# One slot pool, identity-matmul score sums, column-wise layer norm and kept V tiles in a four-layer decode attention kernel

## Chip, cores and metric

The kernel runs on one core of a Trainium2 chip. The metric is the device time of one execution in microseconds (us), as the median of several runs; lower is better. Engines in the profile: PE is TensorE (PEld its weight loads), DVE is VectorE, ACT is ScalarE, POOL is GpSimd, SP is the engine that issues the transfers (SPq its queue). I number layers 1 to 4 and heads 0 to 31; K31 is the K tile of head 31.

## The reference, cut to what matters

```python
# B = Sq = 1, D = 640, 32 heads, 8192 keys, head size 192, bf16
def block(x, k_cache, v_cache, wq, wo):
    q = (x @ wq).reshape(32, 192)
    p = softmax(einsum("hd,hkd->hk", q, k_cache) * 192 ** -0.5)
    return einsum("hk,hkd->hd", p, v_cache).reshape(1, 6144) @ wo
for w in (A, B, A, B):                       # two sets of caches and weights, each used twice
    x = x + block(layernorm(x), *w)
```

A K or V tile of one head is 8192 x 192 bf16, 3.146 MB. Four layers of 32 heads read 256 such tiles and 62.9 MB of Wq and Wo, 868.2 MB in all. Nothing can be reused within a layer, but layers 3 and 4 read the same K and V as layers 1 and 2.

## The kernel before

A tile lies in SBUF as 128 partitions of 64 keys x 192. DVE multiplies the K tile by q, then halves it by adds (192 to 96, 48, 24, 12) for 56 of the 64 key columns and reduces the rest; ACT sums the other 8. PE does the softmax's small transposes and 64 matmuls with V. There are three slots for K, three for V, and two buffers each for Wq and Wo.

```python
e = DV.op(lambda v: v.tensor_tensor(k3, k3, qb_ap, ALU.mult))            # L463, whole tile
...
e = DV.op(lambda v: v.tensor_tensor(kt[:, :, 0:hw_], kt[:, :, 0:hw_], kt[:, :, hw_:DH], ALU.add))   # L492, then L504 x3
...
cur["s"] = DV.op(lambda v: v.tensor_reduce(s_sb[par][:, JA:JJ], kt[:, :, 0:w], AX.X, ALU.add))      # L508
...
for j in range(JJ):                                                       # L557, 64 matmuls with V
    t.matmul(OB[par][0:1, 0:DH], lhsT=p_sb[par][:, j:j + 1], rhs=vs3[:, j, :], ...)
...
# order of the transfers, head by head: K runs one head ahead of V
need_k(h); need_k(h + 1); need_k(h + cfg.get("klead", max(1, NKSLOT - 2))); need_v(h)
...
# weights: rows of 2,048 bytes (Wq, 1,024 columns) and of 1,280 bytes (Wo)
WQ[:, c0:c0 + ncols].rearrange("(c p) n -> p c n", p=128)
WO[r0:r0 + NT * 128, :].rearrange("(t p) n -> p t n", p=128)
```

## Time and profile before

2,074.88 us (2,074.28 to 2,074.90, three runs); the profiled execution spans 2,073.2 us.

From the page of the kernel before: the span, busy time by engine, the rows in 40 slices for PE's granted clock (tenths), the DMA engines (tenths busy) and their rate, then the data queue and the bytes read.

```profile
span 2073.2 us, 24389 instructions
PE 1158.3 (56%) x9625; PEld 915.1 (44%) x9668; DVE 1764.8 (85%) x1190; ACT 596.1 (29%) x3254; POOL 3.1 (0%) x13
PEclk7777777877678777777767777777776777777877
DMA  9999999999999999999999999999999999999995
GB/s 395 430 425 428 422 422 427 426 430 419 423 426 425 427 422 424 426 426 428 418 423 426 423 429 424 422 427 426 426 410 425 425 423 424 423 423 425 426 427 254
q1 hardware_dynamic: 77700, 868.24, 99.3%
HBM read 868.22 MB, written 0.00 MB: 419 GB/s over the span
```

The DMA row is full from the first slice to the last but one: the kernel is bound by its transfers. DVE is busy 85% of the time, but the transfers do not run short because of it.

From the table of stretches of the kernel before; the last two columns are the DMA engines' busy share and the rate in GB/s, the number before them is the granted clock.

```profile
900.00:920.00 20.00, 14.07 (x104) 11.03 (x105) 18.95 (x13) 8.10 (x45) 0.00 (x0) 0.67 1.00 430
920.00:940.00 20.00, 13.66 (x124) 10.82 (x122) 15.13 (x12) 5.54 (x31) 0.00 (x0) 0.90 1.01 420
1540.00:1560.00 20.00, 15.36 (x141) 12.24 (x139) 6.26 (x13) 3.99 (x22) 0.00 (x0) 0.84 0.96 394
```

430 GB/s is the rate with K and V alone; with a weight block in the stretch it is 420 at the same busy share, and at a layer end (the third line) it is lower because the queue runs short for a moment. The Trainium skill, "DMA: Bandwidth & Descriptors", Specifications, puts the fabric ceiling at 435 GB/s; the trace agrees with 430.

From the landing of K31 to the end are 2,073.2 - 2,043.45 = 29.7 us.

### The profile page before, as it was taken

What the parts mean: (1) busy time and instruction counts of PE and PEld (TensorE: products, weight loads), DVE (VectorE), ACT (ScalarE), POOL (GpSimd) and SP (SyncE); (2) the same over time, 40 slices, a digit from 0 to 9 for tenths busy, and PEclk for the clock granted to TensorE, in tenths of its full rate; (3) what the DMA queues carried; (4) which work ended last, traced back from release to release, by engine and by line L of the source; (5) the groups of instructions that cost most, each with busy time, mean ns of one, the idle gap of its engine ahead of it and who ended that gap; (6) DMA issues with size and microseconds to landing.
All of it is one profiled execution on the core that took longest, in us unless ns stands there. A gap on an engine that the chain in (4) does not pass through costs nothing.

```text
span 2073.2 us, 24389 instructions
## 1 busy us (share of the span) xinstructions
PE 1158.3 (56%) x9625; PEld 915.1 (44%) x9668; DVE 1764.8 (85%) x1190; ACT 596.1 (29%) x3254; POOL 3.1 (0%) x13
## 2 busy tenths in 40 slices
PE   2565556555465555566536565556563665556656
PEld 1444444444354444444425454445452454444444
DVE  7888888988698888898779888889878988888896
ACT  2222232232232322232223332223222332223232
POOL 0000000000000000000000000000000000000000
PEclk7777777877678777777767777777776777777877
DMA  9999999999999999999999999999999999999995
GB/s 395 430 425 428 422 422 427 426 430 419 423 426 425 427 422 424 426 426 428 418 423 426 423 429 424 422 427 426 426 410 425 425 423 424 423 423 425 426 427 254
DMA packets 77813, 869.79 MB, mean 420 GB/s; under 512 B 4994, under 2 KB 29572, under 8 KB 44932
## 3 DMA queue, kind: packets, MB, share of 16 engines
q1 hardware_dynamic: 77700, 868.24, 99.3%
q8 instruction: 76, 1.25, 0.2%
q14 instruction: 37, 0.30, 0.0%
HBM read 868.22 MB, written 0.00 MB: 419 GB/s over the span
## 4 chain that ended last, share of the span: by engine, by line
DMA 45%; issue 25%; DVE 24%; PE 4%; ACT 1%; SPq 1%; POOL 0%; POOLq 0%; DVEq 0%; ACTq 0%
DMA kslot<-in_B_k_cache_dram 28%; DMA kslot<-in_A_k_cache_dram 17%; DVE kslot L463 12%; DVE kslot L504 5%; DVE kslot L492 4%; PE OB L557 3%; DVE s_sb L508 1%; SPq L312 0%; DVE M_sb L530 0%; DVE m_sb L515 0%; PE QB L412 0%; PE YL L632 0%; ACT p_sb L547 0%; DVE rl_sb L572 0%; SPq L295 0%
## 5 line engine op out<-in xcount | busy, mean ns | idle before, releaser
L463 DVE TENSOR_TENSOR kslot<-kslot,q_sb 128x12288 bf16<-128x12288 bf16 x128 | 839.3, 6557 | 226.2 <-DMA kslot<-in_A_k_cache_dram 116.6
L557 PE MATMUL OB<-vslot,p_sb 128*1 128x192 bf16 x8192 | 951.1, 294 | 84.3 <-ACT p_sb L547 78.6
L557 PEld LDWEIGHTS OB<-vslot,p_sb 128*1 128x1 bf16 x8192 | 809.6, 101 | 205.7 <-ACT p_sb L547 93.5
L539 PE MATMUL SA<-M_bf,ones_bf 1*128 1x1 bf16 x128 | 22.9, 179 | 689.2 <-ACT M_bf L537 689.2
L504 DVE TENSOR_TENSOR kslot<-kslot 128x2688 bf16<-128x2688 bf16 (+2 forms) x384 | 374.4, 975 | 13.3
L492 DVE TENSOR_TENSOR kslot<-kslot 128x5376 bf16<-128x5376 bf16 x128 | 374.7, 2927 | 0.1
L481 ACT ACTIVATE kslot<-kslot 128x192 bf16<-128x192 bf16 x1024 | 355.3, 348 | 22.2 <-DVE kslot L463 22.2
L539 PEld LDWEIGHTS SA<-M_bf,ones_bf 1*128 1x128 bf16 x128 | 12.4, 97 | 725.0 <-ACT M_bf L537 725.0
L537 ACT ACTIVATE M_bf<-M_sb 1x1 bf16<-1x1 f32 x128 | 26.5, 207 | 666.3 <-DVE M_sb L530 666.3
L481 ACT ACTIVATION_READ_ACCUMULATOR kslot<-kslot 128x1 f32 x1024 | 192.1, 188 | 0.0
L508 DVE TENSOR_REDUCE s_sb<-kslot 128x56 f32<-128x672 bf16 x128 | 109.1, 852 | 4.4
L632 PE MATMUL YL<-wo,oT_sb 128*1 128x512 bf16 x256 | 83.0, 378 | 51.8 <-ACT oT_sb L609 31.7
L605 ACT ACTIVATE oT_sb<-OB 128x1 bf16<-128x1 f32 x64 | 11.2, 175 | 310.9 <-PE OB L593 310.9
L608 ACT ACTIVATE oT_sb<-OB 64x1 bf16<-64x1 f32 x64 | 10.9, 170 | 281.0 <-PE OB L597 281.0
L412 PE MATMUL QB<-wq,xT_b 128*128 128x512 bf16 x197 | 57.5, 426 | 11.2 <-issue 6.4
L523 PE MATMUL SA<-ident,m_bf 128*1 128x128 bf16 x128 | 28.2, 221 | 54.5 <-ACT m_bf L520 54.5
L632 PEld LDWEIGHTS YL<-wo,oT_sb 128*1 128x1 bf16 x256 | 20.7, 81 | 79.7 <-ACT oT_sb L609 37.2
L634 PE MATMUL YH<-wo,oT_sb 128*1 128x128 bf16 x256 | 55.9, 218 | 0.0
L425 ACT ACTIVATE q_sb<-QB 128x512 bf16<-128x512 f32 x48 | 28.7, 598 | 93.6 <-PE QB L412 93.6
L578 ACT ACTIVATE orow_bf<-OB,rl_sb 1x192 bf16<-1x192 f32 x128 | 51.0, 399 | 1.7 <-DVE rl_sb L572 1.7
L547 ACT ACTIVATE p_sb<-s_sb,negm_sb 128x64 bf16<-128x64 f32 x128 | 44.8, 350 | 4.1
L530 DVE TENSOR_REDUCE M_sb<-SA 1x1 f32<-1x128 f32 x128 | 34.7, 271 | 12.6 <-PE SA L523 12.6
(50 smaller groups left out, 368.9 us busy)
## 6 DMA issues: line engine op xcount, KB each, us to landing
kslot<-in_A_k_cache_dram SPq DMA_DIRECT2D x64, 3072.0 KB, 32.6
vslot<-in_A_v_cache_dram SPq DMA_DIRECT2D x64, 3072.0 KB, 36.1
kslot<-in_B_k_cache_dram SPq DMA_DIRECT2D x64, 3072.0 KB, 32.6
vslot<-in_B_v_cache_dram SPq DMA_DIRECT2D x64, 3072.0 KB, 36.3
wq<-in_A_wq_dram SPq DMA_DIRECT2D x12, 1280.0 KB, 24.9
wo<-in_A_wo_dram SPq DMA_DIRECT2D x16, 960.0 KB, 38.2
wq<-in_B_wq_dram SPq DMA_DIRECT2D x12, 1280.0 KB, 25.7
wo<-in_B_wo_dram SPq DMA_DIRECT2D x16, 960.0 KB, 38.6
```

Source lines behind the costliest of these rows:

```text
L412: return t.matmul(QB[nb % 2][:, 0:ncols], lhsT=xT_b[:, c, :], rhs=wq_buf[s_][:, c, (nb % 2) * 512:(nb % 2) * 512 + ncols], start=(c == 0), ...
L463: e = DV.op(lambda v, k3=k3, qb_ap=qb_ap: v.tensor_tensor(k3, k3, qb_ap, ALU.mult))
L481: ea = AC.op(lambda a, k3=k3, par=par, j=j: a.activation(k3[:, j, :], k3[:, j, :], ACT.Copy, accum_out=s_sb[par][:, j:j + 1]))
L492: e = DV.op(lambda v, kt=kt, hw_=hw_: v.tensor_tensor(kt[:, :, 0:hw_], kt[:, :, 0:hw_], kt[:, :, hw_:DH], ALU.add))
L504: e = DV.op(lambda v, kt=kt, hw_=hw_, w=w: v.tensor_tensor(kt[:, :, 0:hw_], kt[:, :, 0:hw_], kt[:, :, hw_:w], ALU.add))
L508: cur["s"] = DV.op(lambda v, kt=kt, par=par, w=w, JA=JA: v.tensor_reduce(s_sb[par][:, JA:JJ], kt[:, :, 0:w], AX.X, ALU.add))
L539: cur["negM"] = PE.op(lambda t, par=par: t.matmul(SA[par][:, SA_NEGM:SA_NEGM + 1], lhsT=ones_bf[0:1, 0:128], rhs=M_bf[par][0:1, 0:1], star ...
L547: cur["p"] = AC.op(lambda a, par=par: a.activation(p_sb[par][:], s_sb[par][:], ACT.Exp, bias=negm_sb[par][:], scale=C))
L557: return t.matmul(OB[par][0:1, 0:DH], lhsT=p_sb[par][:, j:j + 1], rhs=vs3[:, j, :], start=(j == 0), stop=(j == JJ - 1))
L578: cur["orow"] = AC.op(lambda a, par=par: a.activation(orow_bf[par][:], OB[par][0:1, 0:DH], ACT.Copy, scale=rl_sb[par][0:1, 0:1]), tag=(f"O ...
L632: return t.matmul(YL[0:1, 0:512], lhsT=lhsT, rhs=rhs[:, 0:512], start=st, stop=sp_)
L634: return t.matmul(YH[0:1, 0:D - 512], lhsT=lhsT, rhs=rhs[:, 512:D], start=st, stop=sp_)
```

## The change

Intent: fewer bytes (four V tiles of the first two layers stay in SBUF for the last two), longer rows for Wq and Wo, less DVE work (scores summed by PE with an identity matrix), a short layer norm in column form, and one pool of eight slots for everything. The whole kernel was rewritten; its core, condensed (cuts marked by three dots, lines in words shortened):

```diff
-kslot x3, vslot x3, wq_buf x2, wo_buf x2
+slot = [sb(f"slot{i}", [P, J * DH], BF16) for i in range(NSLOT)]        # NSLOT = 8
+KEPT_A = (4, 12)        # V tiles of layer 1 kept until layer 3
+KEPT_B = (20, 28)       # V tiles of layer 2 kept until layer 4
+first(("k", l, h))                                                      # order: K_h, V_h, K_h+1, V_h+1
+if l < 2 or h not in kept[l % 2]:
+    first(("v", l, h))
-DV: multiply whole tile, four halving adds, reduce; ACT: 8 row sums
+for c in range(4):                                                      # DVE: four multiplies of 48 columns
+    v.tensor_tensor(k3[:, :, d0:d0 + QD], k3[:, :, d0:d0 + QD], q..., ALU.mult)
+for c in range(4):                                                      # PE: 24 matmuls of 512 columns
+    for r in range(QD // R):
+        t.matmul(S[:, :], lhsT=ident[:], rhs=k3[:, :, d0:d0 + R], start=..., stop=...)
+v.tensor_reduce(s_sb[par][:], S[:].rearrange("p (j r) -> p j r", r=R), AX.X, ALU.add)
-Wq: 1,024 columns per block; Wo: four heads per block, "(t p) n -> p t n"
+Wq: 1,920 columns (ten heads) per block, "(p c) n -> p c n"; Wo: ten heads, "(p i) n -> p (i n)"
+q and the output projection: bursts of 75 pairs of weight load and one-column matmul per ten heads
-layer norm on one row of 640
+layer norm on 128 x 5, sums over partitions by a matmul with ones
... (launch and helpers cut)
```

With R = 8 an identity matmul reads 64 x 8 columns, so it adds eight of the 192 product columns for all 64 keys at once.

## The prediction

> **What bounds it now.** The DMA engines. The page's DMA row reads 9 in every slice but the last, the data queue is busy 99.3% of the span, 868.2 MB are read. In a table of 20 us stretches the rate is 430 GB/s where only K and V move, 411 to 421 where a Wq (1,280 KB, rows of 2 KB) or Wo (960 KB, rows of 1.3 KB) block is among them. The Trainium skill, "DMA: Bandwidth & Descriptors", Specifications, gives a fabric ceiling of 435 GB/s; the trace agrees: 430. DVE (85%) has slack: it waits 213 us for K (wait list). Data flows from 3 to 2,052 us; then a tail of 21 us.
>
> **Removed, added, moved.**
> 1. Bytes: four V tiles are not read again, 4 x 3.146 = 12.6 MB, at 430 GB/s: -29 us, all critical.
> 2. Row sizes: 56 weight transfers cost about 0.5 us each beyond their bytes (20 us at 420 against 430), 27 us in all. Now there are 32, most with rows of 3.8 KB (Wq) or 19 KB (Wo). I estimate 8 us left: -19 us.
> 3. Tail: 29.7 us lie between the last K's landing and the end. Now: multiply (6.6 us) with identity matmuls behind it, softmax, 64 V matmuls (5.4 us in the last head), a short projection: an estimated 21, so -9 us.
> 4. DVE: the halving tree (2.93 + 1.56 + 0.86 + 0.51 us) and ACT's 8 row sums (4.3 us) go; about 8.5 us of DVE per head stay of 13.8. Off the critical path.
> 5. PE gains 24 identity matmuls of 512 columns per head, and about 150 weight-load-and-matmul pairs per ten heads. At full clock: identity 5.2 us, V 5.4, softmax bubble 2.5, the rest 1.5: an estimated 14.6 us per head against 15.6 us of DMA. So PE becomes nearly critical. The Trainium skill, "TensorE: Matmul & The Clock Gate", Part 1, says that idleness of about 3.4 us halves PE's clock; the trace agrees: 64 V matmuls took 8.3 us starting at a granted 0.5 and 5.44 at 1.0. With pauses under 3 us the clock should stay mostly at 1.0; the PEclk row should rise from 7 to about 9.
> 6. Slots: kept tiles leave four of eight slots for streaming from head 28 of layer 2 to head 4 of layer 3, a Wq block among them, just where projection, norm and q are serial (about 8 us of lag). Bursts at heads 10 and 20 hold PE 5 to 10 us. Estimated +8 us of DMA gaps.
>
> **Sum.** 2,075 - 29 - 19 - 9 + 8 = about 2,026; allowing for better overlap at layer ends **2,022 us**, range **2,006 to 2,062**. Chances: faster by over 2% (below 2,033) **0.70**, within 2% **0.20**, slower **0.10**.
>
> **What would show each step.** (1) 855.7 MB read. (2) Rate near 428 GB/s while data flows. (3) Last K to end about 21 us. (4) DVE busy near 1,100 us. (5) PE busy over 85%, PEclk 9 or 10, identity matmuls some 216 ns apart. (6) DMA dips only at layer ends, the third deepest; the chain of waits still mostly K transfers.
>
> **What would make it wrong.** Identity matmuls read columns in 16-byte pieces with a stride of 384 bytes; no trace shows their rate. If it is lower, or the clock falls to half between heads, PE needs 17 to 20 us per head and the time goes to 2,200 us or more, PE in the chain of waits. If four slots are too few, the DMA row shows gaps through layers 2 and 3 and the result is within 2%. If short rows cost less than I read, step 2 gains only some 10 us.

## More of the kernel before

The end of the kernel before, from its timeline: when K31 and the two last V tiles were issued (the second number is the time that issuing took), the multiply of K31 when it had landed, and the output's transfer.

```profile
2010.75 3.14 SPq L312 DMA_DIRECT2D kslot<-in_B_k_cache_dram  x1
2013.93 13.02 SPq L320 DMA_DIRECT2D vslot<-in_B_v_cache_dram  x2
...
2043.45 6.56 DVE L463 TENSOR_TENSOR kslot<-kslot,q_sb 128x12288 bf16<-128x12288 bf16 x1 [0.77 <-DMA kslot<-in_B_k_cache_dram]
...
2071.65 0.26 SPq L708 DMA_DIRECT2D out_dram<-xout_bf  x1
```

Note the order: K31 is issued ahead of **both** V30 and V31.

## The result

2,049.76 us (2,046.69 to 2,052.19, four runs) against 2,074.78: 25 us or 1.2% faster, within 2%. I had forecast 2,022 us, 53 us faster: the result lies inside the range that I gave, but only 25 of the 53 us came. Ratios given below are the mean time of one kernel's runs over that of the other's of the same rounds, so not quite the ratio of the medians that I quote; here 0.9877 with a 95% interval of 0.9863 to 0.9891. The experiments ran in several rounds; the median of the kernel before lies between 2,074.8 and 2,075.6 us in all of them, so medians of different rounds can be compared to about 1 us. The changed kernel itself scatters more, from 2,046.7 to 2,052.2 us.

The page of the changed kernel, the same lines, then two of its groups (busy us, mean ns of one | idle before).

```profile
span 2050.1 us, 30175 instructions
PE 1669.0 (81%) x13970; PEld 1119.8 (55%) x13970; DVE 1031.3 (50%) x1071; ACT 148.5 (7%) x541; POOL 3.1 (0%) x13
PEclk9998998998899899899889989989989998998998
DMA  9999999999999999999989999999999999999994
GB/s 403 430 430 424 431 428 424 430 431 429 424 430 430 426 428 429 414 431 430 393 349 429 430 426 428 429 424 429 428 431 426 429 429 426 429 428 427 430 428 179
q1 hardware_dynamic: 49376, 855.66, 98.0%
HBM read 855.64 MB, written 0.00 MB: 417 GB/s over the span
...
L368 PE MATMUL S<-slot,ident 128*128 128x512 bf16 x3072 | 741.4, 393 | 115.6 <-DVE rl L410 67.2
L402 PE MATMUL O<-slot,p_sb 128*1 128x192 bf16 x8192 | 794.2, 264 | 0.0
```

What was hoped for is there: 12.6 MB less, and the median slice reads 429 instead of 425. But two slices in the middle fall to 393 and 349, and the last reads 179 instead of 254. That is where a good part of the gain went.

From the table of stretches of the changed kernel: one in mid-layer, then the end of layer 2.

```profile
900.00:920.00 20.00, 17.16 (x111) 10.05 (x111) 11.80 (x12) 1.06 (x4) 0.00 (x0) 0.91 1.00 430
1000.00:1020.00 20.00, 10.34 (x53) 4.51 (x51) 8.03 (x8) 1.37 (x5) 0.00 (x0) 0.74 0.84 347
1020.00:1040.00 20.00, 18.10 (x191) 13.78 (x190) 8.18 (x9) 0.85 (x3) 0.00 (x0) 0.83 0.99 410
1040.00:1060.00 20.00, 13.75 (x94) 7.75 (x91) 9.84 (x18) 1.76 (x6) 0.55 (x1) 0.83 0.80 318
1060.00:1080.00 20.00, 18.10 (x214) 14.04 (x213) 8.47 (x9) 1.34 (x5) 0.00 (x0) 0.91 0.85 350
```

The busy share of the DMA engines falls with the rate: they have nothing to do. And the end of the changed kernel, from its timeline.

```profile
1974.91 0.33 SPq L196 DMA_DIRECT2D slot<-in_B_v_cache_dram  x1
1982.53 0.33 SPq L196 DMA_DIRECT2D slot<-in_B_k_cache_dram  x1
1987.90 0.33 SPq L196 DMA_DIRECT2D slot<-in_B_v_cache_dram  x1
...
2019.08 3.16 PE L331 MATMUL YB<-oT,slot 128*128 128x1 bf16 x75 [0.28 <-ACT oT L326]
2019.14 1.76 DVE L354 TENSOR_TENSOR slot<-slot,q_sb 128x3072 bf16<-128x3072 bf16 x1 [2.05 <-DMA slot<-in_B_k_cache_dram]
...
2022.17 8.04 PE L402 MATMUL O<-slot,p_sb 128*1 128x192 bf16 x64
2030.14 5.35 PE L368 MATMUL S<-slot,ident 128*128 128x512 bf16 x24
2037.68 7.09 PE L402 MATMUL O<-slot,p_sb 128*1 128x192 bf16 x64
2047.03 0.35 SPq L433 DMA_DIRECT2D out_dram<-x_bf  x1
```

Now V30 is issued ahead of K31. K31 lands at 2,019.1; PE is in the third output projection, then does V30 (8.04 us), and comes to K31's identity matmuls only at 2,030.1. The last landing of K is followed by 31.0 us.

### Where the time lies: one account for all runs

To compare traces I count the time that is lost against 430 GB/s. A stretch of t us that moves b MB loses t - b/0.430. The span is then the bytes at 430 GB/s, plus what is lost at the start (first 24 us), within 60 us of the three layer ends, elsewhere in the flow, and in about the last 60 us (the tail). The numbers are sums over 12 us stretches of each profile, in us; they include some 1.5 MB of instruction fetches.

| profile of | span | bytes at 430 | start | layer ends | rest of flow | tail |
|---|---|---|---|---|---|---|
| before | 2073.2 | 2022.4 | 3.8 | 7.4 | 17.8 | 21.7 |
| changed | 2050.1 | 1994.0 | 3.5 | 15.1 | 7.5 | 30.1 |
| keep_none | 2066.1 | 2022.9 | 3.4 | 1.5 | 9.2 | 29.1 |
| keep_a | 2051.2 | 2008.5 | 3.4 | 2.6 | 8.1 | 28.5 |
| keep_b | 2052.3 | 2008.5 | 3.4 | 3.5 | 8.6 | 28.3 |
| wo_short | 2055.6 | 1993.8 | 3.4 | 13.7 | 18.6 | 26.1 |
| before_order | 2080.6 | 2022.4 | 3.7 | 7.6 | 18.2 | 28.7 |

A profile is one execution and lies up to some 4 us off the median of its kernel's timed runs, so I use the table for where time lies and the timed runs for how much.

### The profile page after: what moved, and what is told of

Its sections match the earlier page's. It is cut to its first block, busy times and chain, and to the rows that moved or that the text cites. A ratio compares the mean times of both kernels' runs of the same rounds, so it can differ in the third digit from the quotient of the medians.

```text
span 2050.1 us, 30175 instructions
## 1 busy us (share of the span) xinstructions
PE 1669.0 (81%) x13970; PEld 1119.8 (55%) x13970; DVE 1031.3 (50%) x1071; ACT 148.5 (7%) x541; POOL 3.1 (0%) x13
## 2 busy tenths in 40 slices
DMA packets 49500, 857.57 MB, mean 418 GB/s; under 512 B 4832, under 2 KB 7392, under 8 KB 15584
## 3 DMA queue, kind: packets, MB, share of 16 engines
HBM read 855.64 MB, written 0.00 MB: 417 GB/s over the span
## 4 chain that ended last, share of the span: by engine, by line
PE 45%; DMA 40%; DVE 11%; ACT 2%; issue 1%; another core or an unknown queue 1%; SPq 0%; ACTq 0%; DVEq 0%
DMA slot<-in_A_k_cache_dram 23%; PE O L402 20%; PE S L368 20%; DMA slot<-in_B_k_cache_dram 17%; DVE slot L354 7%; DVE s_sb L371 2%; PE YB L331 2%; ACT p_sb L381 1%; DVE negm L379 1%; PE TB L289 1%; PE MX L376 1%; DVE m_bf L375 1%; PE MX L385 1%; PE TB L323 1%
## 5 line engine op out<-in xcount | busy, mean ns | idle before, releaser
L354 DVE TENSOR_TENSOR slot<-slot,q_sb 128x3072 bf16<-128x3072 bf16 x512 | 872.3, 1741 | 534.9 <-DMA slot<-in_A_k_cache_dram 300.8
L368 PE MATMUL S<-slot,ident 128*128 128x512 bf16 x3072 | 741.4, 393 | 115.6 <-DVE rl L410 67.2
L402 PE MATMUL O<-slot,p_sb 128*1 128x192 bf16 x8192 | 794.2, 264 | 0.0
L402 PEld LDWEIGHTS O<-slot,p_sb 128*1 128x1 bf16 x8192 | 723.9, 90 | 42.1
L368 PEld LDWEIGHTS S<-slot,ident 128*128 128x128 bf16 x3072 | 289.1, 101 | 517.0 <-DVE slot L354 190.4
L371 DVE TENSOR_REDUCE s_sb<-S 128x64 f32<-128x512 f32 x128 | 88.5, 692 | 396.6 <-PE S L368 396.6
L381 ACT ACTIVATE p_sb<-s_sb,negm 128x64 bf16<-128x64 f32 x128 | 44.5, 348 | 904.5 <-DVE negm L379 904.5
L315 ACT ACTIVATE q_sb<-QB 128x192 bf16<-128x192 f32 x120 | 39.6, 330 | 774.3 <-PE QB L308 774.3
L413 ACT ACTIVATE orow<-O,rl 1x192 bf16<-1x192 f32 x128 | 51.4, 402 | 129.0 <-PE O L402 67.6
L331 PE MATMUL YB<-oT,slot 128*128 128x1 bf16 x900 | 37.9, 178 | 3.3 <-ACT oT L326 3.3
L375 DVE TENSOR_REDUCE m_bf<-s_sb 128x1 bf16<-128x64 f32 x128 | 28.5, 222 | 4.4
L289 PE MATMUL TB<-xb,slot 128*128 128x1 bf16 x900 | 26.1, 165 | 4.2 <-issue 2.8
L308 PEld LDWEIGHTS QB<-ident,qT 128*128 128x128 bf16 x240 | 13.7, 97 | 20.5 <-issue 20.5
## 6 DMA issues: line engine op xcount, KB each, us to landing
slot<-in_B_v_cache_dram SPq DMA_DIRECT2D x62, 3072.0 KB, 30.1
```

The source lines that it names most:

```text
L289: e = PE.op(lambda t, b=b, c=c: t.matmul(TB[:, C_QT + b:C_QT + b + 1], lhsT=t3[:, c, b * P:(b + 1) * P], rhs=xb[:, c:c + 1], start=(c == 0 ...
L331: e = PE.op(lambda t, i=i, c=c, f=y_first[0], fin=fin: t.matmul(YB[:, c:c + 1], lhsT=t3[:, i, c:D:DC], rhs=oT[:, i:i + 1], start=f, stop=f ...
L354: e = DV.op(lambda v, d0=d0: v.tensor_tensor(k3[:, :, d0:d0 + QD], k3[:, :, d0:d0 + QD], q_sb[qi][:, d0:d0 + QD].unsqueeze(1).broadcast_to ...
L368: e = PE.op(lambda t, d0=d0, fin=fin: t.matmul(S[:, :], lhsT=ident[:], rhs=k3[:, :, d0:d0 + R], start=(d0 == 0), stop=fin), signal=fin)
L371: e = DV.op(lambda v: v.tensor_reduce(s_sb[par][:], S[:].rearrange("p (j r) -> p j r", r=R), AX.X, ALU.add), e, last["s"][par])
L375: ev_m = DV.op(lambda v: v.tensor_reduce(m_bf[par][:], s_sb[par][:], AX.X, ALU.max), e, last["m"][par])
```

## The experiments

Theory: (1) the slots that kept tiles hold make the transfers run short at the end of layer 2 and eat most of the second pair's saving; (2) the tail grew because the order of the last transfers changed and because PE does the last heads' work strictly in order. Rivals: the layer end is a serial chain whatever the slots; the tail is PE's sheer amount of work, or drifting DMA engines; the rate gain in mid-layer has nothing to do with row sizes.

### How many tiles to keep

The edits are in two lines of the changed kernel.

```diff
-KEPT_A = (4, 12)
-KEPT_B = (20, 28)
+KEPT_A = ()   KEPT_B = ()            # keep_none
+KEPT_A = (4, 12)   KEPT_B = ()       # keep_a
+KEPT_A = ()   KEPT_B = (20, 28)      # keep_b
```

> The changed kernel with no V tile kept: 868.2 MB again. Theory A (the kept tiles cost back what they save: with four of eight slots held, the transfers stall for some 14 us at the end of layer 2, and bytes saved late in the last layer only lengthen the tail): about +29 us of bytes, -12 us of stall, -4 to -8 us of tail, so 2,059 to 2,063 us against 2,050, and the dips at the second layer end in the DMA row gone. Rival B (the stall is the serial chain at a layer end and has nothing to do with slots; every byte lies on the path): about 2,079 us, and the dips at 1,000 to 1,080 us stay.

Measured 2,069.15 us, ratio to before 0.9970 (0.9956 to 0.9983).

> Only the two A tiles kept (heads 4 and 12 of layers 1 and 3), 861.9 MB; at the end of layer 2 six slots stream instead of four. Theory A: +14.6 us of bytes, -11 us of stall, -3 to -5 us of tail: 2,047 to 2,051 us, the same as with four tiles kept. Rival B: 2,064 us.

Measured 2,053.69 us, ratio 0.9895 (0.9882 to 0.9909).

> Only the two B tiles kept (heads 20 and 28 of layers 2 and 4), 861.9 MB. Theory A: +14.6 us of bytes, -11 us of stall, tail as long as now: about 2,053 us, so somewhat slower than keeping A alone, because the bytes saved lie at the end of the last layer. Rival B: 2,064 us, as with A alone.

Measured 2,054.76 us, ratio 0.9903 (0.9890 to 0.9917).

The end of layer 2 in keep_a, the same four stretches as shown of the changed kernel:

```profile
1000.00:1020.00 20.00, 11.91 (x100) 6.39 (x98) 8.65 (x9) 1.37 (x5) 0.00 (x0) 0.79 1.01 432
1020.00:1040.00 20.00, 18.10 (x169) 13.81 (x168) 7.55 (x9) 0.85 (x3) 0.00 (x0) 0.87 1.00 420
1040.00:1060.00 20.00, 13.75 (x147) 7.78 (x145) 11.97 (x20) 1.77 (x7) 0.55 (x1) 0.81 1.01 428
1060.00:1080.00 20.00, 18.10 (x161) 13.84 (x160) 11.49 (x11) 1.39 (x6) 0.00 (x0) 0.93 0.97 406
```

With six slots free instead of four the same serial chain at the layer end (PE's columns are nearly alike) costs the DMA engines almost nothing. So part (1) holds. At the second layer end alone (60 us to both sides) the loss is 0.4 us in keep_none, 1.7 in keep_a, 0.9 in keep_b and 13.8 in the changed kernel; the two other layer ends lose 0.4 to 1.8 us each in all four. Two kept tiles bring 15.5 us (2,069.15 to 2,053.69), about what 6.3 MB take at 430 GB/s (14.6 us), and the next two only some 4 us of 14.6 (2,053.69 to 2,049.76, or to 2,049.39 in after_again below). The rival, which foresaw 2,079 and 2,064 us, falls. My guess that bytes saved late in the last layer (the B tiles) are worth less than the A tiles is not shown: the 1 us between keep_a and keep_b is inside the spread. My own figures missed too, by 6 us in keep_none and by 2 to 3 in keep_a and keep_b: in the first two I had expected the tail to shrink by 3 to 8 us, and it shrank by 1.0 and 1.6.

### Which heads' tiles

```diff
-KEPT_A = (4, 12)
+KEPT_A = (0, 1)
```

> Four tiles kept, but the A tiles are those of heads 0 and 1 instead of 4 and 12: the same bytes, and four tiles are held at once only from head 28 of layer 2 to head 1 of layer 3 (three only until then, two after). Theory A (held slots make the stall at the end of layer 2): the stall of 14 us falls to 5 to 9 us: 2,041 to 2,045 us. If what counts is that four are held at the layer end itself, it stays: 2,049 us.

Measured 2,049.04 us, ratio 0.9873 (0.9859 to 0.9888): as the changed kernel. The layer ends lose 13.1 us (15.1 in the changed kernel, 13.6 when it was run again), not the 5 to 9 that I had expected at the second. What counts here is that four tiles are held across the layer end itself, not for how long.

### Row sizes

```diff
-w["wo"][r0:r0 + HEADS_W * DH].rearrange("(p i) n -> p (i n)", p=P)      # 128 rows of 19,200 bytes
+w["wo"][r0:r0 + HEADS_W * DH].rearrange("(i p) n -> p i n", p=P)        # 1,920 rows of 1,280 bytes
-lhsT=orow[0:1, i:k * P:k]
+lhsT=orow[0:1, i * P:(i + 1) * P]      # the last, small Wo block likewise
```

> Wo read in rows of 1,280 bytes again (as before the change), all else as changed; same bytes. If short rows cost what I read from the trace before (0.49 us per 768 rows beyond their bytes): 12 transfers of 1,920 rows instead of 128, about +14 us: 2,064 us, and dips to some 415 GB/s in the stretches that hold a Wo block. Rival (the row size does nothing, the rate rose because there are fewer transfers): 2,050 us.

Measured 2,058.91 us, ratio 0.9920 (0.9906 to 0.9934): 9.1 us slower than the changed kernel. In the flow the loss is 9.7 us larger (13.7 + 18.6 against 15.1 + 7.5), and the tail is 4 us shorter. The number of transfers is the same in both, so short rows do cost, about two thirds of what I had read from the trace before, and the rival falls.

### The order of the last transfers, in the kernel before

```diff
                 g = h // HG
+                if l == NL - 1 and h == H - 2:
+                    need_v(h)                      # V30 ahead of K31
                 need_k(h); need_k(h + 1); need_k(h + cfg.get("klead", max(1, NKSLOT - 2))); need_v(h)
```

> The kernel before, with one change: in the last layer the V tile of head 30 is asked for ahead of the K tile of head 31, as in the changed kernel. If the order of the last transfers is part of why the changed kernel's tail is longer, the last K lands up to 7 us later and the whole is 4 to 7 us slower: 2,079 to 2,082 us. If the tail is TensorE's or VectorE's work alone, no change: 2,075 us.

Measured 2,082.41 us against 2,075.62 in the same rounds, ratio 1.0033 (1.0020 to 1.0045): 6.8 us slower by one swap of two transfers. The lines that answer to those of the kernel before:

```profile
2001.31 12.73 SPq L320 DMA_DIRECT2D vslot<-in_B_v_cache_dram  x2
2014.09 2.03 SPq L312 DMA_DIRECT2D kslot<-in_B_k_cache_dram  x1
2027.03 0.33 SPq L320 DMA_DIRECT2D vslot<-in_B_v_cache_dram  x1
...
2050.89 6.56 DVE L463 TENSOR_TENSOR kslot<-kslot,q_sb 128x12288 bf16<-128x12288 bf16 x1 [8.04 <-DMA kslot<-in_B_k_cache_dram]
```

K31's multiply starts at 2,050.89 instead of 2,043.45, and the end moves by the same 7.4 us. In the account the tail goes from 21.7 to 28.7 us, nearly the changed kernel's 30.1. K is the tile with the long chain behind it (multiply, sums, softmax), V only has its 64 matmuls, so the last K must come early. By its size this would be the larger part of the tail's growth; the next run tests it in the changed kernel.

### The end order in the changed kernel

```diff
+# last layer: plan K31 ahead of V30 (condensed; the split of head() into parts is cut)
+plan.remove(("k", NL - 1, H - 1)); plan.insert(i_, ("k", NL - 1, H - 1))
+# and PE does head 31's identity matmuls and softmax before the V matmuls of heads 30 and 31
+if l == NL - 1 and h == H - 2:
+    held.append(values); held.append(lambda: finish("o")); return
```

> All as changed but the last two heads of the last layer: the transfers come in the order K30, K31, V30, V31, and TensorE does the identity matmuls and softmax of head 31 before the V matmuls of heads 30 and 31. Theory S (what sets the tail is the in-order chain behind the last K: it waits behind V of head 30, then 5.3 us of identity matmuls, 2.2 of softmax, 5.4 of V): the last K lands some 7 us earlier and only V matmuls stand behind the last data: 2,043 to 2,046 us against 2,050. Rival (TensorE's backlog since head 20 sets the end, whatever the order): 2,049 us or more.

Measured 2,046.89 us, ratio 0.9863 (0.9847 to 0.9880): 2.9 us better by the medians, but the interval overlaps the changed kernel's. K31's multiply now starts at 2,013.8 instead of 2,019.1; the timeline shows that PE can't use it at once: it finishes the third projection first and starts the identity matmuls at 2,018.9, which then take 7.96 us instead of 5.35 because the clock has fallen. From its timeline and its table of stretches, these matmuls and the granted clock (0.50, the third number from the end) while they run:

```profile
2018.93 7.96 PE L373 MATMUL S<-slot,ident 128*128 128x512 bf16 x24
...
2020.00:2024.00 4.00, 4.00 (x10) 1.32 (x9) 0.64 (x1) 0.00 (x0) 0.00 (x0) 0.50 0.23 98
```

The tail is 28.1 us. So in this kernel the order alone does not give back the 7 us: PE's work in order is next in line.

### Less work for PE

```diff
-for c in range(4): multiply chunk c (48 columns); PE: 24 identity matmuls
+multiply chunks 0, 3, 2; add chunk 3 to chunk 2 on DVE; multiply chunk 1; PE: 18 identity matmuls
```

> All as changed, but VectorE adds the last quarter of each product tile to the third (one more add of 3,072 elements, about 1.76 us per head), so TensorE needs 18 identity matmuls per head instead of 24 (1.3 us less). Theory P (TensorE is behind in the last twelve heads and at the end of layer 2, and its backlog is the tail of 30 us and part of the stall of 14 us): tail shorter by 4 to 6 us, stall by 2 to 4 us: 2,040 to 2,045 us. Rival D (slots and transfers alone set stall and tail): 2,049 to 2,052 us, no gain.

Measured 2,052.71 us, ratio 0.9887 (0.9870 to 0.9903): no gain, although a quarter of the identity matmuls is gone. From its page, the granted clock and the two matmul groups (V, then identity):

```profile
PEclk8988898988889789799788979989887897988998
...
L406 PE MATMUL O<-slot,p_sb 128*1 128x192 bf16 x8192 | 863.4, 277 | 0.5 <-issue 0.5
...
L372 PE MATMUL S<-slot,ident 128*128 128x512 bf16 x2304 | 615.2, 419 | 175.4 <-DVE slot L361 121.2
```

The mean clock fell from 0.914 to 0.853, and the V matmuls, which were not touched, rose from 264 to 277 ns each and from 794 to 863 us busy. The identity matmuls rose from 393 to 419. PE's busy time fell by 61 us, where a quarter of 741 would have been 185. The PE that had less to do was granted a lower clock, and two thirds of the saving in busy time were gone. In the account the tail did shrink as expected, from 30.1 to 26.0 us, but the layer ends lost 19.3 us instead of 15.1, so nothing was left.

```diff
+# quarter, and: K31 planned ahead of V30, third projection behind V30's matmuls (last layer)
```

> The quarter version, and in the last layer the last K is transferred ahead of the V before it, and the third projection runs behind head 30's V matmuls instead of ahead of them. Theory P: the last K's multiply is over before TensorE gets to it, so the tail after the last data falls to about 20 us: 5 to 8 us better than the quarter version, 2,033 to 2,039 us. Rival D: as the quarter version.

Measured 2,053.34 us, ratio 0.9894 (0.9879 to 0.9908): no gain either. Here K31 was early, but PE waited 1.8 us for V30 and then did V30 (8.2 us), the projection and only then K31's sums. The tail was 28.9 us, longer than in quarter. The two changes got in each other's way; the run says only that moving the projection behind V30 does not help here.

### Keeping the clock up

```diff
                 freed[nk] = e                      # behind the identity matmuls of a head
+                PE.wait(last["TB"])
+                for _ in range(7):                 # results unused, columns 256 to 511 of a bank
+                    PE.op(lambda t: t.matmul(TB[:, 256:512], lhsT=ident[:], rhs=<ident twice>, start=True, stop=True), signal=False)
```

> All as changed, plus seven matmuls of 256 columns per head on unused PSUM columns, in TensorE's pause between the identity matmuls and the row maximum (about 0.8 us of a pause of 1.0). If short pauses are what makes the granted clock fall (64 V matmuls take 6.96 us in every second head instead of 5.30): PEclk mean from 0.914 to 0.96 or more, most V groups at 5.3 us, and under theory P 3 to 5 us gained: about 2,046 us. If the pause is not the cause, the clock stays at 0.91 and the fillers cost: 2,050 to 2,055 us.

Measured 2,046.61 us, ratio 0.9861 (0.9846 to 0.9875), 3.2 us better by the medians, intervals overlapping. From its page:

```profile
PEclk9998998998899899899989989989988998998999
...
L406 PE MATMUL O<-slot,p_sb 128*1 128x192 bf16 x8192 | 729.9, 252 | 0.0
```

The mean clock is 0.945 instead of 0.914, and the V matmuls are 64 us less busy (730 against 794). Counted over the timelines, 112 of the 128 groups of V matmuls take 5.4 us, against 73 in the changed kernel; the groups of 7.1 us are nearly gone, and the slow ones left all stand behind a burst or at the start of a layer. The tail is 25.1 us. That the pause of some 2 us per head lowers the clock is shown; that it is worth 3 us is likely, not certain.

> The quarter version (18 identity matmuls) with the seven filler matmuls. The quarter version alone gained nothing, and its clock fell from 0.914 to 0.853. If the lower clock ate what the missing matmuls saved, the fillers should give it back: PEclk above 0.91, and clearly faster than the fillers alone (2,046.6): 2,038 to 2,043 us. If TensorE's work does not matter at all, it stays at 2,045 to 2,049 us.

Both together: 2,049.63 us, ratio 0.9877 (0.9862 to 0.9891). The fillers did bring the clock back to 0.916, but the time is that of the changed kernel. My expectation of 2,038 to 2,043 us was wrong. With the clock as in the changed kernel and PE 76 us less busy (1,593 against 1,669) nothing is gained, which speaks against the rival that the sheer amount of PE work sets the time. DVE's extra add also delays the last identity matmuls of each head, and I have no run that takes the two apart.

### Depth of the queue

```diff
         def transfer(n):
+            if len(landed) >= 3:
+                SP.wait(list(landed.values())[-3])
```

> All as changed, but a transfer is issued only when the third one before it has landed, so at most three are in flight. At the end of the changed kernel the rate is half (some 220 GB/s) for about 10 us: as if half the DMA engines had run ahead. Theory Q (a deep queue lets engines drift apart, and that puts off the last K's landing): the half-rate phase shrinks to under 6 us and some 3 us are gained, about 2,047 us. Rival (the drift is harmless, or the slow engines set the pace anyway): 2,049 to 2,055 us.

Measured 2,051.24 us, ratio 0.9884 (0.9869 to 0.9899): no gain, and the time at about half rate at the end is hardly shorter. Limiting the queue to three transfers does not remove that stretch (more of it in the last section), and it costs in the flow, which loses 11.1 us instead of 7.5.

### Together

> The end order of the last two heads, the A tiles of heads 0 and 1, and the fillers together. If the three are separate losses the gains add (about 5, 6 and 4 us): 2,033 to 2,038 us. If they draw on the same slack, not below 2,042 us.

End order, A tiles of heads 0 and 1, and fillers: 2,046.57 us, ratio 0.9861 (0.9846 to 0.9876). The gains do not add. The layer ends still lose 13.4 us, the tail 24.7, as with the fillers alone.

> The changed kernel again, unaltered, as a yardstick on this chip: 2,047 to 2,052 us, ratio 0.986 to 0.989.

The changed kernel: 2,049.39 us, ratio 0.9874 (0.9860 to 0.9887), as before.

```diff
+# endswap and warm7, and inside each burst of 75 one-column matmuls seven more fillers (the expectation says eight)
+if b % 2 == 0 and b < NW - 1:
+    PE.op(lambda t: t.matmul(TB[:, 256:512], lhsT=ident[:], rhs=<ident twice>, ...), signal=False)
```

> Changed kernel with the end order of the last two heads, the fillers in the pause, and eight more fillers inside each burst of 75 one-column matmuls (projection, q columns). If the idle-looking bursts are what leaves the clock at half for the V or identity matmuls behind them: PEclk mean 0.96 or more, V groups behind a burst at 5.5 us instead of 8.0, and 2,040 to 2,044 us. If the fillers only cost: 2,046 to 2,049 us.

Measured 2,048.22 us, ratio 0.9866 (0.9853 to 0.9880). The fillers inside the bursts did not raise the clock (0.942): they took 370 to 380 ns each there, where the mean of those in the pause is 273. At the pair of bursts that I looked at (head 10 of layer 3) the bursts took 7.9 us instead of 5.1 to the first V matmul, and the V group behind them 6.6 instead of 8.2. They cost at least what they brought.

```diff
+# final_four with KEPT_B = (20,)
```

> As final_four with three tiles kept instead of four (A of heads 4 and 12, B of head 20): +7.3 us of bytes, and five slots at the end of layer 2 instead of four, so the stall of 12 us falls to 2 to 5 us: the same as final_four within 3 us.

Measured 2,049.46 us, ratio 0.9874 (0.9859 to 0.9889), the same within 3 us. The layer ends lose 7.5 us with three tiles, 16.2 with four in final_four, 1.5 to 3.5 with two or none: the loss grows as the free slots go from six (or eight) to four.

No version is clearly better than the changed kernel; warm7, endswap and combo are at 2,046.6 to 2,046.9 us in their rounds, all clear of the kernel before.

## Why the prediction was wrong, point by point

| step | forecast, us | measured, us | from |
|---|---|---|---|
| 1 bytes | -29 | -28.4 | account, bytes at 430 |
| 2 row sizes | -19 | -8.6 | rest of flow, before (17.8) to keep_none (9.2) |
| 3 tail | -9 | +8.4 | account, 21.7 to 30.1 |
| 6 gaps | +8 | +11.9 | layer ends and rest of flow, keep_none (10.7) to changed (22.6) |
| better overlap at layer ends | -4 | -5.9 | layer ends, before (7.4) to keep_none (1.5) |
| start | 0 | -0.3 | account |
| sum | -53 | -22.9 | spans: -23.1; medians: -25 |

**Step 3 failed, and it is 17 of the 30 us missed** (step 2 makes 10 of the rest and step 6 makes 4; the layer ends gave 2 back). The text said: "Tail: 29.7 us lie between the last K's landing and the end. Now: ... an estimated 21, so -9 us." Two things were wrong with it. First, I took it that the last K lands at the same distance from the end of the data as before. It does not: the kernel before issues K31 ahead of V30, the changed one behind it. Put into the kernel before, that order alone costs 6.8 us (before_order; 7.0 in the tail). Second, the chain behind the last K is 31.0 us, not 21. I let the identity matmuls run right behind the multiply, but PE works in order: it did the third projection and V30 first, and started on K31 11.0 us after it landed, after which all 24 identity matmuls took their full 5.35 us. That is 16.3 us where I had about 8. V31 took 7.09 us instead of 5.4 at the lower clock, and the output transfer of 128 rows of 10 bytes took 3.1 us from its issue to the end (2,047.03 to 2,050.1) where the one row before took 1.6. The two parts, 7.0 and 31.0 - 29.7 = 1.3, make up the 8.4 us but for rounding. The first is shown in the kernel before; in the changed kernel, undoing it (endswap) brought only 2.9 us, because PE was then the next to be late.

**Step 6: mechanism right, size too small.** The gaps came where I said, "from head 28 of layer 2 to head 4 of layer 3", and the series of kept tiles (none, two, three, four) shows that the slots cause them. I allowed 8 us; they are 11.9. In effect the second pair of kept tiles saves 14.6 us of bytes and pays about 11 back. I should have asked for each pair what it brings and what it holds. The list of signs says "the third deepest", which counted wrongly: the deep dip is at the second of the three layer ends.

**Step 2: mechanism right, size too large.** -8.6 us instead of -19, or -14.5 instead of -23 together with the layer ends, from which the split at 60 us does not part it cleanly. keep_none differs from the kernel before in much else, so as an effect of row size only wo_short's 9.1 us for Wo is shown. With Wo's rows short, the rest of the flow loses as much as in the kernel before (18.6 and 17.8 us): for the longer rows of Wq nothing is left in the account, and no run tests them alone.

**Step 1: right.** 855.64 MB read.

**Step 4: nearly right.** DVE is busy 1,031 us (forecast near 1,100). It is not quite off the critical path: it makes up 11% of the chain that ended last, after 24% before.

**Step 5: mostly right on durations, wrong on the clock.** 24 identity matmuls take 5.19 us in the chain of waits where PE is the one that is late (5.34 in the timeline, which counts the last one to its end), 216 ns each, although they read 16-byte pieces with a stride of 384 bytes; that risk did not come true. The Trainium skill, "TensorE: Matmul & The Clock Gate", "Wait — 56ns, not 53.3ns?", gives 215.7 ns for 512 columns, and the trace agrees. But I wrote "With pauses under 3 us the clock should stay mostly at 1.0". The mean is 0.914, and 64 V matmuls take 5.4 us in 73 of the 128 heads, about 7.1 in most of the others, often every second or third, and 8.0 behind a burst of one-column matmuls (2,022.17 in the changed kernel's end above). PE was busy 81%, not over 85. From the timeline of the changed kernel, three heads in which PE is late:

```profile
577.45 5.44 PE L402 MATMUL O<-slot,p_sb 128*1 128x192 bf16 x64
582.92 5.34 PE L368 MATMUL S<-slot,ident 128*128 128x512 bf16 x24
590.44 7.09 PE L402 MATMUL O<-slot,p_sb 128*1 128x192 bf16 x64
597.57 5.34 PE L368 MATMUL S<-slot,ident 128*128 128x512 bf16 x24
605.09 1.15 PE L402 MATMUL O<-slot,p_sb 128*1 128x192 bf16 x12
```

Where PE is late a head takes 13.0 us (577.45 to 590.44) or 14.7 (590.44 to 605.09). A K and a V tile take 6.29 MB / 0.430 = 14.6 us. So PE keeps up but makes up lost time only slowly, and the chain of waits became 45% PE and 40% DMA; I had said "still mostly K transfers".

**Still open.** Why the small gains of end order and clock do not add up; fillers alone and all together end at the same 2,046.6 us. The traces show a tail near 25 us in both and PE at work in it with only short pauses, but no run isolates what sets those 25 us.

## What to carry to other kernels

When a kernel is bound by transfers, ask of a tile kept on chip not only what it saves but which buffers it holds when the next serial point comes: here the first two kept tiles brought their whole 15 us and the next two a quarter of theirs. At the end of the program, order the last transfers by the length of the work behind them, not by the order of use: one swap was worth 6.8 us in the kernel before, and some 3 in the changed one (not clear of its noise), where PE came late as well. And cost a tail engine by engine in program order, with what each still has to finish when the last data lands.

## What the Trainium skill lacked or had wrong

- "TensorE: Matmul & The Clock Gate", "HAM oscillation", gives as the rule that PE should have no idle gaps above some 3.4 us. That is not enough: here PE pauses for 1.04 and 0.86 us within a head, 1.9 us in all, and the clock still fell, often in every second or third head (64 V matmuls 5.44 or 7.09 us); filling 0.8 us of the pause raised the mean clock from 0.914 to 0.945. The page's next section, "A second HAM failure mode: psum-queue depth-cycling", does say that frequent micro-idles make the clock oscillate, but gives no length for them. The difference of 1.65 us agrees with the page's window (Part 1) of about 3.4 us: at half clock that is an estimated 1.7 us.
- The same page does not say how one-column matmuls count. 75 pairs of weight load and one-column matmul kept PE busy for 3.2 us by the profile, but the granted clock fell to 0.5 within the burst, and the 64 V matmuls behind them took 8.0 us, as after idleness (8.29 us in the kernel before, at 2,051.32). The pauses just before the burst may have a share in it; no run takes them apart.
- The same page gives no figure for how far the clock falls when work is taken off PE: with 18 instead of 24 identity matmuls (and one more add on DVE ahead of the last of them) the mean clock went from 0.914 to 0.853.
- "DMA: Bandwidth & Descriptors", Specifications, gives 512 bytes as the size from which transfers run at line rate. Rows of 1,280 instead of 19,200 bytes (3,840 in the small blocks) cost 9.1 us over the 12 large Wo blocks and the four small ones (29.5 MB and 2.0 MB), with both sizes above 512. Its section "Why small descriptors are slow" does have a fixed cost of about 3 cycles per packet, worked out for 256 bytes only. By the profile wo_short moved 22,528 packets more than the changed kernel (72,028 and 49,500), so an estimate from these runs is 9.1 x 16 / 22,528 = 6.5 ns per packet on each of the 16 engines.
- The page does not give a number for how far the 16 DMA engines drift apart. In the changed kernel the rate is half for some 8 us at the end, as if some engines were done while others still had work; the engines were not looked at one by one. The lines are of the table of stretches, busy share and rate at the end:

```profile
2016.00:2020.00 4.00, 2.34 (x41) 2.09 (x42) 1.59 (x4) 0.63 (x3) 0.00 (x0) 1.00 0.52 221
2020.00:2024.00 4.00, 4.00 (x68) 3.61 (x67) 4.00 (x4) 0.00 (x0) 0.00 (x0) 0.59 0.52 219
```

  The kernel before shows it too (276 and 154 GB/s between 2,048 and 2,056 us), so it is not what the change brought; whether and why the engines drift is open.
